# Four u tiles from TensorE to the DMA crossbar, and another order in the SyncE queue

## The chip, the cores and the metric

The kernel runs on one core of one Trainium2 chip. A core has five engines with a program each: TensorE (PE, matrix products), VectorE (DVE), ScalarE (ACT), GpSimd (POOL) and SyncE (SP). SyncE and GpSimd also issue DMAs, each from a queue of its own that works strictly in its program's order. The metric is device time in microseconds, the median over several runs. An engine waits for another through semaphores; whatever is next in its program waits behind the waiting instruction.

## The reference

A causal attention with a sliding window of 64, then a low-rank mixing along the sequence, then a two-layer MLP, both with a residual:

```python
scores = scale * np.matmul(q, k.transpose(0, 1, 3, 2))   # 8 batches, 8 heads, 576 x 64
mask = (rel >= 0) & (rel < 64)
attn = softmax(np.where(mask, scores, -1e9))
x = np.matmul(attn, v).transpose(0, 2, 1, 3).reshape(B, S, 512)
h = x.transpose(0, 2, 1) @ U @ V                          # rank 32, along the sequence
u = x + h.transpose(0, 2, 1)
out = u + np.maximum(u @ w_ch1, 0.0) @ w_ch2              # 512 -> 2048 -> 512
```

Inputs and output are float32; the kernel computes in bf16 with float32 accumulation.

## The kernel before

The 8 x 576 = 4608 tokens are seen in two ways. The attention and the mixing go by batch (576 tokens, four and a half tiles of 128). The MLP goes by chunk: nine chunks of 512 tokens, four tiles each, tile number g = 0 to 35. Batch b begins in tile g0 = floor(4.5 b), so batch 1 has its tiles t = 0 to 4 at g = 4 to 8, batch 2 has t = 0 to 3 at 9 to 12, batch 3 has t = 0 to 4 at 13 to 17. Chunk 2 is made of g = 8 to 11 (the last tile of batch 1 and three of batch 2), chunk 3 of g = 12 to 15 (the last of batch 2 and t = 0 to 2 of batch 3).

The program is one software pipeline with a schedule written out by hand. `mlp(c)` gives 32 steps for chunk c, here called groups: 16 products with W1, each 4 matmuls of 128x128 by 128x512 into a PSUM tile `psA` (line 765), whose relu goes to DVE or ACT by the lists `DVE_RELU` (775, 777); then, for each of the four output tiles, four quarters of the product with W2 into `psU` (789), a residual sum on DVE (802) and a store (815). Each group has a slot number, 0 to 31. After the group of a slot comes what the tables `PLACE...` put in that slot: the pieces of batch b = c + 1. A number above 100 means a slot of the next chunk. All engines get their instructions in that one order.

The pieces of a batch are:

- `T`: k and q with the head dimension on the partitions. Batches 0 and 1 do it on TensorE. From batch 2 on it is five `TX(t)`, each with two crossbar transposes (DMA) of SyncE, kf<-kr and qf<-qr (line 306). Their slots stand in `CROSS`: in chunk 1, for example, batch 3's at slots 10 to 14 and batch 4's at 26 to 30.
- `S`, `M`: scores (347; the short last block first, into `low` and `high`), exponential on ACT (367, 400), mask multiply on DVE (373, 380).
- `SV`: shifted copies of v, `vB`, on ACT and DVE (149, 152).
- `PV`: probabilities times v (409) and the division on DVE (490 to 512), into `xs`.
- `U`, `V`: the two low-rank products (533, 542; 660), and the sum with x on DVE (675) that gives a u tile `un`. The V product of a whole batch is made in one slot, by `mixed`: before the change in the order tile 4, tiles 0 and 1, tiles 2 and 3, and DVE sums in the same order. Tile 4 uses one bank of each of two other PSUM pools (`two_banks`).
- `UT(t)`: u with the model dimension on the partitions, `uTc`, which is what the W1 groups read. For batches below `NXT` = 3 it is four TensorE transposes into the PSUM tile `tpu` (694) and a copy on ACT (697). From batch 3 on it is one crossbar transpose on SyncE (690).

In chunks 1 and 2 the first W1 group is made in two pieces, three tiles and then the fourth, so that the last `uTc` tile may come a little later.

SyncE's queue has the transposes of k and q, those of u and the output stores, each waiting for its data in program order. GpSimd's queue has the loads of k, q and v from DRAM (128, 137), which cast float32 to bf16. `loads(b, t)` holds them back: a one-element copy `held` on GpSimd (963) reads tile t of the transposed q of batch b + 1, so that it waits for that transpose to land; behind it in the queue come the loads of v of batch b + 1 (for b = 1 and 2) and of k and q of batch b + 2. A second `held` (974), in later chunks, waits for the fourth `uTc` tile of the running chunk before the v loads of the next batch. k and q of a batch land in the buffers `kr`, `qr` that batch b - 2 had; the transposed ones in `kf`, `qf`, two of each.

Of the kernel before, what the change touches and what calls it, by code (L numbers as in the profile page):

```python
# [16 lines left out]
def kernel(  # L17
# [12 lines left out]
    B, H, S, D = q.shape  # L30
# [11 lines left out]
    NGR = 2  # L42
    NXB = 2
    NXT = 3
    FOLD = {0: 0, 1: 0, 2: 1, 3: 1}
    GP = S // GR
    NFULL = S // P
    CH = 512
    TPC = CH // P
# [32 lines left out]
    NT = 5  # L82
# [172 lines left out]
    def attention(b, spare=False):  # L255
# [11 lines left out]
        grouped = b < NGR  # L267
        folded = FOLD.get(b, 2)
        turn = [0]
# [415 lines left out]
        def UT(t):  # L685
            def f():
                g = g0 + t
                dst = uT_of(g // TPC)[:, g % TPC, :, :]
                if b >= NXT:
                    nc.sync.dma_start_transpose(out=dst, in_=u_tiles[g][:])  # L690
                    return
                tp = ps_tp.tile([P, NDC, P], BF16, name="tpu", tag="tp")
                for dc in range(NDC):
                    nc.tensor.transpose(  # L694
                        tp[:, dc, :], u_tiles[g][:, dc * P : (dc + 1) * P], ident[:]
                    )
                nc.scalar.copy(out=dst, in_=tp[:])  # L697
            return f
# [13 lines left out]
        if spare:  # L712
            pcs["L"] = [PVL(t) for t in range(2)]
            pcs["R"] = PVR
            pcs["XT"] = [XT(t, range(NDC if t < 2 else 2)) for t in range(NFULL)]
            pcs["idle"] = idle_turns
            pcs["X3"] = [XT(t, (2, 3)) for t in (2, 3)]
            pcs["HT"] = [HT((0, 1)), HT((2, 3))]
            pcs["V"] = [f for ts in ((0, 1), (2, 3), (4,)) for f in VM(ts)]
        else:  # L720
            def two_banks():
                return (
                    psum["mm"].tile([P, CH], FP32, name="psv0", tag="mm"),
                    ps_tp.tile([P, CH], FP32, name="psv1", tag="tp"),
                )

            def mixed(parts=None):
                parts = parts or [VM((NT - 1,), two_banks), VM((0, 1)), VM((2, 3))]
                for part in parts:
                    part[0]()  # L730
                for part in parts:
                    for add in part[1:]:
                        add()

            pcs["V"] = [mixed]
            if b == 1:

                def last():
                    for f in VM((NT - 1,)):
                        f()  # L740

                pcs["V"] = [lambda: mixed([VM((0, 1)), VM((2, 3))]), last]
            pcs["UT"] = [UT(t) for t in range(NT if odd else NT - 1)]
        return pcs


    DVE_RELU = {0: (7, 9, 11, 15), 1: (4, 7, 9, 10, 11, 13, 14)}
    DVE_RELU_N = (0, 1, 2, 4, 5, 6, 14)

    def mlp(c):  # L750
        uTc = uT_of(c)
        c1 = [None] * NFC

        def ch1(*ids):
            def f():
                if len(ids) == 1:
                    ps = {ids[0]: psum["mm"].tile([P, CH], FP32, name="psA", tag="mm")}
                else:
                    pair = ps_big.tile([P, 2, CH], FP32, name="psA", tag="big")
                    ps = {i: pair[:, n, :] for n, i in enumerate(ids)}  # L760
                parts = (slice(0, TPC - 1), slice(TPC - 1, TPC)) if c in (1, 2) and ids == (0,) else (slice(0, TPC),)
                for ts in parts:
                    for dc in range(NDC):
                        for i in ids:
                            nc.tensor.matmul(  # L765
                                ps[i][:, ts.start * P : ts.stop * P],
                                w1b[:, dc, i * P : (i + 1) * P],
                                uTc[:, ts, dc, :],
                                start=(dc == 0),
                                stop=(dc == NDC - 1),  # L770
                            )
                for i in ids:
                    c1[i] = c1_pool.tile([P, CH], BF16, name=f"c1_{i}")
                    if i in DVE_RELU.get(c, DVE_RELU_N):
                        nc.vector.tensor_relu(out=c1[i][:], in_=ps[i][:])  # L775
                    else:
                        nc.scalar.activation(out=c1[i][:], in_=ps[i][:], func=ACT.Relu)  # L777
            return f

        acc = {}  # L780

        def ch2(t, quarter, parts=((0, DM),)):
            def f():
                g = c * TPC + t
                for lo, hi in parts:
                    if quarter == 0 or len(parts) > 1:
                        acc[t] = psum["mm"].tile([P, DM], FP32, name="psU", tag="mm")
                    for i in range(4 * quarter, NFC if len(parts) > 1 else 4 * quarter + 4):
                        nc.tensor.matmul(  # L789
                            acc[t][:, lo:hi],  # L790
                            c1[i][:, t * P : (t + 1) * P],
                            w2b[:, i, lo:hi],
                            start=(i == 0),
                            stop=(i == NFC - 1),
                        )
                    if quarter < 3 and len(parts) == 1:
                        continue
                    if c < NLATE:
                        osb = late[c * TPC + t]
                    else:  # L800
                        osb = out_pool.tile([P, DM], FP32, name="osb")
                    nc.vector.tensor_tensor(  # L802
                        out=osb[:, lo:hi],
                        in0=acc[t][:, lo:hi],
                        in1=u_tiles[g][:, lo:hi],
                        op=ALU.add,
                    )
                    if c < NLATE:
                        stores.append(
                            lambda: nc.sync.dma_start(  # L810
                                out=outf[g * P : (g + 1) * P, :], in_=osb[:]
                            )
                        )
                        continue
                    nc.sync.dma_start(out=outf[g * P : (g + 1) * P, lo:hi], in_=osb[:, lo:hi])
            return f

        ups = [ch1(i) for i in range(NFC)]
        if c == 0:
            ups[0:2] = [ch1(0, 1), lambda: None]  # L820
            rest = [ch2(t, r) for r in range(4) for t in (0, 1)]
            return ups + rest + [ch2(t, r) for t in (2, 3) for r in range(4)]
        rest = [ch2(t, r) for t in range(TPC) for r in range(4)]
        if c == NCH - 1:
            rest[-4:] = [ch2(TPC - 1, 0, ((0, 3 * P), (3 * P, DM)))]
        return ups + rest


    PLACE = {
        "S": [0, 0, 0, 3, 3],  # L830
        "M": [0, 1, 2, 4, 5],
        "PV": [8],
        "U": [14],
        "V": [18],
        "UT": [19, 19, 20, 20, 21],
    }
    PLACE_0 = {"V": [0, 0, 1, 2, 2, 3, 4, 4, 4]}
    PLACE_1 = {
# [7 lines left out]
        "UT": [28, 29, 30, 31, 102],  # L846
    }
    PLACE_2 = {
        "S": [9, 9, 9, 12, 12],
        "M": [9, 10, 11, 13, 14],  # L850
        "SV": [15, 15, 16, 16],
        "PV": [18],
        "U": [23],
        "V": [25],
        "UT": [28, 29, 30, 31],
    }
    PLACE_3 = {**PLACE, "SV": [5, 5, 6, 6], "V": [16], "UT": [17, 17, 18, 18, 19]}
    CROSS = {
        0: {2: [16, 17, 18, 19, 20]},
        1: {3: [10, 11, 12, 13, 14], 4: [26, 27, 28, 29, 30]},  # L860
        2: {5: [24, 25, 26, 27, 28]},
    }
    CROSS_N = [22, 23, 24, 25, 26]
# [81 lines left out]
    for c in range(NCH):  # L945
        slots = all_slots[c]
# [8 lines left out]
        b = c + 1  # L955
        if b < B:
# [4 lines left out]
            def loads(b, *tiles):  # L961
                for t in tiles:
                    nc.gpsimd.tensor_copy(  # L963
                        out=held[:],
                        in_=qfs[(b + 1) % 2][0:1, t * HP * P : t * HP * P + 1],
                    )
                if b <= 2:
                    load_v(b + 1)
                for _ in load_kq(b + 2, False):
                    pass  # L970
# [5 lines left out]
            if 2 < b and b + 2 < B:  # L976
                loads(b, 2)
            where = {1: PLACE_1, 2: PLACE_2, 3: PLACE_3}.get(b, PLACE)
            if b < NXB:
# [23 lines left out]
            if b == 1:  # L1003
                slots[20].append(lambda: loads(1, 2))
            if b == 2:
                slots[15].append(lambda: loads(2, 2))
        for fill, extra in zip(mlp(c) + [lambda: None], slots):
            fill()
            if c == NCH - 2 and stores:
# [33 lines left out]
```

The softmax here doesn't subtract the row's maximum and nothing guards it: scores larger than these inputs give would overflow.

## Time and profile before

| | us |
|---|---|
| median of 13 runs | 311.18 (310.94 to 313.27) |
| the profiled execution | 310.99 |
| its span in the profile | 309.0 |
| TensorE busy | 302.3 (98%) |
| DVE / ACT / GpSimd busy | 174.4 / 108.3 / 102.0 |
| chunk 1 starts / chunk 2 / chunk 3 / chunk 4 | 59.56 / 92.64 / 124.43 / 155.99 |

The page gives the busy time of each engine, and the span in 40 slices; the chain of waits is the sequence of work that ended last, followed back from the last instruction; a timeline lists instructions of one engine with their start, their length and, in brackets, how long the engine was idle before and what ended that. A DMA's "us to landing" is counted from the start of its issue to its completion. Line numbers are those of the kernel before; in the changed kernel they are one higher from line 45 on.

### The profile page before, as it was taken

What the parts mean: (1) busy time and instruction counts of PE and PEld (TensorE: products, weight loads), DVE (VectorE), ACT (ScalarE), POOL (GpSimd) and SP (SyncE); (2) the same over time, 40 slices, a digit from 0 to 9 for tenths busy, and PEclk for the clock granted to TensorE, in tenths of its full rate; (3) what the DMA queues carried; (4) which work ended last, traced back from release to release, by engine and by line L of the source; (5) the groups of instructions that cost most, each with busy time, mean ns of one, the idle gap of its engine ahead of it and who ended that gap; (6) DMA issues with size and microseconds to landing.
All of it is one profiled execution on the core that took longest, in us unless ns stands there. A gap on an engine that the chain in (4) does not pass through costs nothing.

```text
span 309.0 us, 6974 instructions
## 1 busy us (share of the span) xinstructions
PE 302.3 (98%) x2903; PEld 147.1 (48%) x2903; DVE 174.4 (56%) x336; ACT 108.3 (35%) x173; POOL 102.0 (33%) x136
## 2 busy tenths in 40 slices
PE   7989999999999999999999999999999999999996
PEld 6643554544445544454445444544454444444443
DVE  4585467527757773677567765766566542116011
ACT  3745670458128610642054304430344004101500
POOL 8693264294399091519233705000000000000000
PEclk9999999999999999999999999999999999999999
DMA  7999999999999999999999999933300275011011
GB/s 107 165 210 208 205 171 142 158 131 156 129 150 156 135 150 148 205 152 152 155 154 116 190 129 125 179 104 85 122 2 0 68 236 192 34 68 36 0 66 69
DMA packets 156495, 39.87 MB, mean 129 GB/s; under 512 B 145040, under 2 KB 151440, under 8 KB 156464
## 3 DMA queue, kind: packets, MB, share of 16 engines
q0 software_dynamic: 104720, 18.88, 84.4%
q1 hardware_dynamic: 51744, 20.55, 36.0%
q8 instruction: 22, 0.36, 0.5%
q14 instruction: 9, 0.07, 0.1%
HBM read 37.97 MB, written 9.44 MB: 153 GB/s over the span
## 4 chain that ended last, share of the span: by engine, by line
PE 93%; DMA 3%; POOL 2%; issue 1%; DVE 0%; POOLq 0%
PE psA L765 41%; PE psU L789 41%; DMA vA<-in_v_dram 3%; PE sc L347 3%; PE xw L409 2%; PE psv L660 1%; PE pshh L533 1%; PE tpu L694 1%; PE tpg L283 0%; POOL qr L120 0%; PE low L347 0%; PE psh L533 0%; POOL vB L152 0%; PE xr L409 0%; POOL kr L120 0%
## 5 line engine op out<-in xcount | busy, mean ns | idle before, releaser
L765 PE MATMUL psA<-uTc,w1b 128*128 128x512 bf16 (+1 forms) x584 | 131.2, 377 | 0.3 <-DVE uTc L635 0.3
L789 PE MATMUL psU<-w2b,c 128*128 128x512 bf16 (+2 forms) x592 | 128.9, 373 | 0.0
L789 PEld LDWEIGHTS <-c 128*128 128x128 bf16 x592 | 56.0, 98 | 66.1 <-issue 3.1
L765 PEld LDWEIGHTS <-w1b 128*128 128x128 bf16 x584 | 54.4, 98 | 63.9 <-issue 2.6
L777 ACT ACTIVATE c<-psA 128x512 bf16<-128x512 f32 x84 | 50.0, 597 | 83.6 <-PE psA L765 83.3
L775 DVE TENSOR_SCALAR c<-psA 128x512 bf16<-128x512 f32 x60 | 41.4, 690 | 40.9 <-PE psA L765 40.9
L802 DVE TENSOR_TENSOR osb<-psU,un 128x512 f32<-128x512 f32 (+2 forms) x29 | 19.5, 671 | 51.9 <-PE psU L789 51.9
L367 ACT ACTIVATE pts<-sc 128x1024 bf16<-128x1024 f32 x32 | 31.4, 1030 | 2.4 <-PE sc L347 2.3
L138 POOL DMA_DIRECT2D vA<-in_v_dram x32 | 28.3, 912 | 7.3 <-DMA w1b<-in_moe_w_ch_dram 2.7
L675 DVE TENSOR_TENSOR un<-psv,xs 128x512 bf16<-128x512 f32 (+3 forms) x48 | 26.1, 593 | 5.5 <-PE psv L660 5.3
L129 POOL DMA_DIRECT2D qr<-in_q_dram x30 | 26.8, 895 | 3.8 <-PE sc L347 1.7
L129 POOL DMA_DIRECT2D kr<-in_k_dram x30 | 26.6, 887 | 3.5 <-PE psA L765 2.0
L400 ACT ACTIVATE ptl<-low 128x256 bf16<-128x256 f32 x6 | 2.3, 383 | 60.5 <-PE high L347 60.5
L373 DVE TENSOR_TENSOR pts<-pts,maskA 128x1024 bf16<-128x1024 bf16 x28 | 19.1, 682 | 1.7 <-ACT pts L367 1.7
L500 DVE TENSOR_TENSOR xs<-xw,rcw 128x896 bf16<-128x896 f32 x14 | 15.3, 1092 | 0.5
L963 POOL COPY held<-qf 1x1 bf16<-1x1 bf16 x5 | 0.9, 177 | 42.9 <-DMA qf<-qr 42.9
L347 PEld LDWEIGHTS <-kf 64*64 64x64 bf16 x704 | 9.9, 107 | 7.4 <-issue 6.4
L347 PE MATMUL sc<-qf,kf 64*64 64x128 bf16 (+1 forms) x608 | 11.7, 212 | 0.5 <-DVE qf L300 0.3
L409 PEld LDWEIGHTS <-pts 128*64 128x64 bf16 x512 | 9.9, 110 | 3.8 <-issue 2.9
L697 ACT COPY uTc<-tpu 128x512 bf16<-128x512 bf16 x9 | 5.3, 585 | 11.1 <-PE tpu L694 11.1
L409 PE MATMUL xw<-vA,pts 128*64 128x65 bf16 x217 | 8.4, 195 | 0.0
L138 POOL DMA_DIRECT2D vB<-in_v_dram x8 | 7.3, 907 | 2.8 <-DMA qr<-in_q_dram 2.4
(125 smaller groups left out, 180.8 us busy)
## 6 DMA issues: line engine op xcount, KB each, us to landing
out_dram<-osb SPq DMA_DIRECT2D x27, 256.0 KB, 2.4
vA<-in_v_dram POOLq DMA_DIRECT2D x32, 128.0 KB, 7.6
kr<-in_k_dram POOLq DMA_DIRECT2D x24, 128.0 KB, 5.7
qr<-in_q_dram POOLq DMA_DIRECT2D x24, 128.0 KB, 5.7
w2b<-in_moe_w_ch_dram POOLq DMA_DIRECT2D x4, 512.0 KB, 15.8
out_dram<-late SPq DMA_DIRECT2D x8, 256.0 KB, 4.1
vB<-in_v_dram POOLq DMA_DIRECT2D x8, 128.0 KB, 8.8
w1b<-in_moe_w_ch_dram POOLq DMA_DIRECT2D x2, 512.0 KB, 10.8
```

Of the source, the lines that this page charges most:

```text
L129: nc.gpsimd.dma_start(out=dst[0:rows, t, :, :], in_=src[b, :, t * P : t * P + rows, :].rearrange("h p d -> p h d"),)
L138: nc.gpsimd.dma_start(out=dst[:, :, 0:D], in_=v[b, :, lo : lo + P, :].rearrange("h p d -> p h d"))
L347: nc.tensor.matmul(sc[g][r0 : r0 + W, col * W : (col + n) * W], keys_of(j, u, rs), queries_of(j, blk, n, rs), start=not spare, stop=last o ...
L367: nc.scalar.activation(out=dst, in_=sc[:], func=ACT.Exp, scale=scale)
L373: nc.vector.tensor_tensor(out=dst, in0=dst, in1=maskA.rearrange("p g n w -> p g (n w)"), op=ALU.mult)
L409: nc.tensor.matmul(dst, pts[:, h // 2, h % 2, blk, :] if blk < NB - 1 else ptl[:, h // 2, h % 2, :], rhs, start=True, stop=True,)
L675: nc.vector.tensor_tensor(out=u_tiles[g][rs, cs], in0=ps[0][n][rs], in1=x[rs, t, :, :].rearrange("p h d -> p (h d)")[:, cs], op=ALU.add,)
L765: nc.tensor.matmul(ps[i][:, ts.start * P : ts.stop * P], w1b[:, dc, i * P : (i + 1) * P], uTc[:, ts, dc, :], start=(dc == 0), stop=(dc == ...
L775: nc.vector.tensor_relu(out=c1[i][:], in_=ps[i][:])
L777: nc.scalar.activation(out=c1[i][:], in_=ps[i][:], func=ACT.Relu)
L789: nc.tensor.matmul(acc[t][:, lo:hi], c1[i][:, t * P : (t + 1) * P], w2b[:, i, lo:hi], start=(i == 0), stop=(i == NFC - 1),)
L802: nc.vector.tensor_tensor(out=osb[:, lo:hi], in0=acc[t][:, lo:hi], in1=u_tiles[g][:, lo:hi], op=ALU.add,)
```

## The change

A table `XUT` names four u tiles below batch 3 that now take the crossbar: tile 4 of batch 1, tiles 0, 1 and 3 of batch 2. `mixed` makes tiles 0 to 3 ahead of tile 4. Batch 2's pieces move one to five slots forward in chunk 1; the `UT` of batch 3 and of later batches one slot or two. Two of batch 4's five `TX` move from slots 29 and 30 of chunk 1 to slot 17 of chunk 2, which is after the `UT` of batch 3's tiles 0 to 2 (slot 16) and before those of its tiles 3 and 4 (slot 18). `held` in chunk 1 reads tile 4 of batch 3's transposed q where it read tile 2. Chunk 2's first W1 group is made in one piece, and chunk 1's relus of DVE are others, the same in number.

```diff
+    XUT = ((1, 4), (2, 0), (2, 1), (2, 3))
...
-                if b >= NXT:
+                if b >= NXT or (b, t) in XUT:
                     nc.sync.dma_start_transpose(out=dst, in_=u_tiles[g][:])
                     return
...
-                parts = parts or [VM((NT - 1,), two_banks), VM((0, 1)), VM((2, 3))]
+                parts = parts or [VM((0, 1)), VM((2, 3)), VM((NT - 1,), two_banks)]
...
-    DVE_RELU = {0: (7, 9, 11, 15), 1: (4, 7, 9, 10, 11, 13, 14)}
+    DVE_RELU = {0: (7, 9, 11, 15), 1: (3, 6, 8, 9, 10, 12, 13)}
...
-                parts = (slice(0, TPC - 1), slice(TPC - 1, TPC)) if c in (1, 2) and ids == (0,) else (slice(0, TPC),)
+                parts = (slice(0, TPC - 1), slice(TPC - 1, TPC)) if (c, ids) == (1, (0,)) else (slice(0, TPC),)
...
     PLACE = {
...
-        "UT": [19, 19, 20, 20, 21],
+        "UT": [18, 18, 19, 19, 20],
...
     PLACE_2 = {
-        "S": [9, 9, 9, 12, 12],
-        "M": [9, 10, 11, 13, 14],
-        "SV": [15, 15, 16, 16],
-        "PV": [18],
-        "U": [23],
-        "V": [25],
-        "UT": [28, 29, 30, 31],
+        "S": [8, 8, 8, 11, 11],
+        "M": [8, 9, 10, 12, 13],
+        "SV": [13, 13, 14, 14],
+        "PV": [15],
+        "U": [20],
+        "V": [22],
+        "UT": [23, 23, 28, 25],
     }
-    PLACE_3 = {**PLACE, "SV": [5, 5, 6, 6], "V": [16], "UT": [17, 17, 18, 18, 19]}
+    PLACE_3 = {**PLACE, "SV": [5, 5, 6, 6], "V": [16], "UT": [16, 16, 16, 18, 18]}
     CROSS = {
         0: {2: [16, 17, 18, 19, 20]},
-        1: {3: [10, 11, 12, 13, 14], 4: [26, 27, 28, 29, 30]},
+        1: {3: [10, 11, 12, 13, 14], 4: [26, 27, 28, 117, 117]},
...
-                slots[15].append(lambda: loads(2, 2))
+                slots[15].append(lambda: loads(2, NT - 1))
```

## The prediction

> **What bounds the kernel now.** I read the page first, then the chain of work that ended last, then the timelines of the SyncE and GpSimd queues with the landing times of their transfers.
>
> ```profile
> span 309.0 us, 6974 instructions
> PE 302.3 (98%) x2903; PEld 147.1 (48%) x2903; DVE 174.4 (56%) x336; ACT 108.3 (35%) x173; POOL 102.0 (33%) x136
> PEclk9999999999999999999999999999999999999999
> PE 93%; DMA 3%; POOL 2%; issue 1%; DVE 0%; POOLq 0%
> ```
>
> TensorE is the bound: 98% busy, the clock full in every slice. The chain's 3% of DMA and 2% of POOL lie in the first 16 us. From 21.9 us on it is TensorE without a hole, so a matmul taken out shortens the run by its length, and a TensorE wait put in lengthens it by its length. Nothing after 22 us can absorb either.
>
> The chain, in order of time (start, us, what, instructions), has the transposes that the change removes, and the place I fear:
>
> ```profile
> 62.34 0.22 PE tpu L694 x4
> ...
> 89.16 0.22 PE tpu L694 x4
> 90.25 0.22 PE tpu L694 x4
> ...
> 92.42 0.22 PE tpu L694 x4
> ...
> 124.43 0.86 PE psA L765 x4
> 125.29 0.14 PE low L347
> ```
>
> The last two lines are the start of chunk 3: its first W1 group, then the scores of batch 4. These scores need the fourth and fifth q and k tiles of batch 4, crossbar-transposed by SyncE.
>
> The GpSimd timeline shows when transposes land, because a `held` copy waits for one and lets the next loads go:
>
> ```profile
> 82.20 0.18 POOL L963 COPY held<-qf 1x1 bf16<-1x1 bf16 x1 [9.12 <-DMA qf<-qr]
> 82.73 3.52 POOL L138 DMA_DIRECT2D vA<-in_v_dram  x4 [0.36 <-DVE rco L508]
> ...
> 107.81 0.18 POOL L963 COPY held<-qf 1x1 bf16<-1x1 bf16 x1 [7.56 <-DMA qf<-qr]
> 108.63 0.87 POOL L129 DMA_DIRECT2D kr<-in_k_dram  x1 [0.65 <-issue]
> ```
>
> And the SyncE timeline (issues; each transposed tile takes SyncE some 1.3 us):
>
> ```profile
> 83.72 1.22 SPq L306 DMA_TRANSPOSE qf<-qr  x1
> 92.04 1.19 SPq L306 DMA_TRANSPOSE kf<-kr  x1
> ...
> 99.28 1.51 SPq L306 DMA_TRANSPOSE qf<-qr  x1
> ...
> 106.39 1.78 SPq L306 DMA_TRANSPOSE qf<-qr  x1
> 112.48 6.25 SPq L690 DMA_TRANSPOSE uTc<-un  x4
> ```
>
> Now batch 4's last transpose is issued at 106.39 and lands 6.4 us later, at 112.8: 12.5 us before the scores at 125.3.
>
> How long a transpose takes depends on the loads around it. Alone it lands in 2.4 us (qf issued at 81.11). The DMA issues of a short window around 112.5 us, with the us to landing at the end:
>
> ```profile
> kr<-in_k_dram POOLq DMA_DIRECT2D x1, 128.0 KB, 6.3
> uTc<-un SPq DMA_TRANSPOSE x1, 6.3
> ```
>
> A load issued at 112.09 and a transpose issued at 112.48 took the same 6.3 us, although nothing was left before that transpose on its own queue (the last one landed at 112.8). So the transfers of both queues are served about in the order of their issue. The price of a place in that line: from the load issued at 92.27 (landed 98.9) to the transpose issued at 106.39 (landed 112.8) lie 7 full loads and 9 transposes in 13.9 us, 0.87 us each; from the load of 108.63 (landed 113.2) to the u tile of 119.42 (landed 125.4) lie 8 loads, 5 transposes and a store in 12.2 us, again 0.87.
>
> **The change, part by part.**
>
> *Four u tiles leave TensorE.* Batch 1's tile 4 and batch 2's tiles 0, 1 and 3: 4 x 0.22 us by the chain's rows = -0.88 us, all of it on the path. ScalarE loses four copies of 0.585 us that nobody waited for: nothing. Chunk 2's first W1 group is no longer split; at chunk 1 the two pieces are 4 matmuls in 0.65 us and 4 in 0.22 us, 0.87 against 0.86 for an unsplit group: nothing.
>
> *The u tiles in time?* Batch 1's tile 4 is ready at 60.4 and goes into SyncE's gap between 62.7 (last transpose of batch 2's q) and 70.5; needed at 91.8. Batch 2's attention comes three groups sooner (3 x 0.86, and 0.22 of removed transposes): its V product at 83.0 instead of 85.8, its first sums at about 83.9, before SyncE is through with batch 3's transposes at 84.9. So SyncE issues tiles 0, 1 and 3 at 85.0, 86.3 and 87.6. GpSimd's loads now start after 86.8 (below), so 2.4 to 5.0 us to landing (5.0 is the row of 83.72, which had loads beside it): tile 1 at 88.7 to 91.3, needed when chunk 2 starts, at 92.64 - 0.88 = 91.8. In time by 0.5 us at worst. Tile 2, still on TensorE, moves two groups forward. Nothing.
>
> *Batch 2's attention sooner.* Its scores start at 67.5; the last transposed q tile lands at 61.45 + 5.3 = 66.8. P times V moves 2.8 us forward, from 77.88 to 75.07, but the last mask multiply (75.41 + 0.68 = 76.1 now) moves only with its scores, one group and 0.22, to 75.0. The slack of 1.8 us is gone; between 0 and 0.3 us of wait, I take +0.1. The seven DVE relus of chunk 1 are renumbered, not added. V products in the order (0,1), (2,3), (4) leave one 128x512 bank of the "mm" pool busy some 2.5 us longer; its next user is two groups (1.7 us) and more behind DVE's 3.1 us of sums, and three banks turn: nothing.
>
> *GpSimd's gate.* `held` in chunk 1 now waits for batch 3's last q tile (issued 83.72) instead of the third (landed 82.1). With no load beside it the last one lands in 2.4 us, at 86.1; the first v load follows 0.68 us later as now, at 86.8 instead of 82.73: +4.1 us. Behind it in GpSimd's queue: five v loads of batch 3, ten q and k loads of batch 4, five v loads of batch 4, the next `held`, and q and k of batch 5. Batch 3's v then lands at 91.4 + 4.1 = 95.5; its shifts come at 98.5: covered. Batch 4's v (110.6 now) is shifted at 117: covered. But batch 4's first k load lands 4.1 us later, so SyncE's transposes of batch 4 begin at 96.1 instead of 92.04, the third q tile is issued at 103.4 and lands at 111.8 instead of 107.7, and batch 5's loads begin at 112.7 instead of 108.63.
>
> *SyncE's order in chunk 2.* Batch 4's tiles 3 and 4 (four transposes) now stand behind batch 3's u tiles 0 to 2. These wait for DVE's sums: V product at 110.72 - 0.88 = 109.8, first sum done 0.9 us later, first issue at 110.9 (before: 112.48, since the halves of tile 4 were summed first). SyncE idles from 104.9 until then. Then 1.3 us each: u tiles at 110.9, 112.2, 113.5, batch 4's k and q tiles at 114.8, 116.1, 117.4 and **118.7**. That last one went at 106.39 before.
>
> When does it land? Batch 5's loads issue from 112.7 on, 0.87 us apart, right among these. Bounds: 2.4 us (alone), at 121.1; and by the line, first load at 112.7 + 4.6 = 117.3, then 6 loads and 5 transposes of 0.87 us: 126.9. The nearest rows are the three u tiles that now go 3.9, 5.2 and 7.0 us after the first load of batch 5: they took 6.3, 7.5 and 8.1 us. The last q tile would be 6.0 us after it: 7.8 us, 126.5. I take this. The scores of batch 4 could start at 125.29 - 0.88 + 0.1 = 124.5. **TensorE waits 2.0 us** there, at the start of chunk 3, with everything of that chunk queued behind in program order. Batch 3's u tiles, which the same chunk needs at 123.7, land by 113.5 + 2.4 to 6.3, before 120: the order helps them by 4 us, which they need only by a hair (the third landed at 123.7 of 124.4).
>
> *Later chunks.* Two u tiles go before a store; they land (2.6 us) 4 us ahead of need, and the second `held` opens up to 3 us sooner, for loads needed 20 us later. Nothing.
>
> **Sum** against the profiled execution, 310.99 us (span 309.0, 2 us around it; the median of the 13 runs is 311.18): -0.88 + 0.1 + 2.0 = +1.2, **312.2 us**.
>
> [...]
>
> **Rivals.**
> 1. *No wait at batch 4's scores.* The transposes overtake the loads: the chunk's -0.88 stays, 310.2 us, faster. For it: v loads issued at 97.95 landed after 12.6 us while a transpose of the same moment (97.87) took 8.3, so in a long backlog transposes do overtake, by up to 4 us; 2 us are enough. Against it: the u tiles of 112 to 116 did not. It decides from a landing before 124.7, a latency under 6.0 us at 118.7.
> 2. *A small wait*, 0.2 to 1.4 us, landing between 124.7 and 125.9 (a latency of 6.0 to 7.2 us): within 0.2% of now, about 311.0. For it speak the u tile of 117.54, with 6.9 us, and the transposes of 92 to 95, with 5.7 to 7.3; against it, that these had fewer transposes ahead of them.
> 3. *The wait is elsewhere*: batch 2's u tile 1 late for chunk 2. If it took the 8.1 us that is the longest of any u tile, it would land at 94.4, 2.6 us late: 310.99 - 0.78 + 2.6 = 312.8. It decides from a latency of 5.4 us; the gate on the loads speaks against it.
> 4. *SyncE slower too*: the four u tiles of 112.48 took 6.25 us, 1.56 each. At that pace the last q tile goes at 120.3 and lands at 128.1: wait 3.6, 313.8 us.
>
> **How the numbers follow.** The measurement tells about 0.2% (0.6 us) from no change. Forecast, with rival 4 in it (a wait over 1.4 us at batch 4's scores): 0.55. Rival 1: 0.25. Rival 2: 0.13. Rival 3: 0.07. Slower 0.55 + 0.07 = 0.62, same 0.13, faster 0.25. The range takes in rival 1 with 0.3 us to spare below and rival 4 above, 309.9 to 313.8; the forecast alone, 311.6 to 313.8.
>
> **What would show it.** 36 - 16 = 20 TensorE transposes of u left. `held` in chunk 1 ending at 86.3, not 82.2. SyncE's last transpose of batch 4 at about 118.7. In the chain, a piece "DMA qf<-qr" or "kf<-kr" of about 2 us before the scores near 124.5. I am wrong if that piece is missing, if q's transposes under batch 5's loads land in less than 6 us, or if the gate's four microseconds are made up before batch 4's third q tile.

## The result: slower by 1.2%

The changed kernel takes **314.81 us** (median of 11 runs, 312.99 to 317.63) against 311.16 for the kernel before (48 runs in all, 310.28 to 313.27): a ratio of **1.012**, 95% interval 1.0101 to 1.0138. The prediction had the sign and the place; its 312.2 us was 2.6 us short, and the result lies above its range.

The profiled execution took 315.28 us, 4.29 more than that of before. The page after:

```profile
span 313.6 us, 6946 instructions
PE 304.0 (97%) x2883; PEld 147.0 (47%) x2883; DVE 174.7 (56%) x336; ACT 106.1 (34%) x169; POOL 101.9 (32%) x136
PEclk9999999999999999799999999999999999999999
PE 88%; DMA 7%; POOL 2%; SPq 1%; issue 1%; DVE 0%; POOLq 0%
```

TensorE has 20 instructions fewer (four transposes of four matmuls, and four matmuls of chunk 2's first group, which is no longer split), and yet is busy 1.7 us longer. The chain has 7% of DMA where it had 3%. And the clock's row, full in all 40 slices before, has a 7 in the seventeenth, which is the stretch from 125.4 to 133.3 us.

Its chain of waits (start, us, what) shows where all this lies:

```profile
61.65 6.25 DMA qf<-qr
67.94 0.19 PE low L348
...
120.86 6.91 DMA qf<-qr
127.81 0.19 PE low L348
128.13 0.46 PE sc L348 x31
128.59 4.38 PE psA L766 x12
```

Three things are new. Batch 2's scores (67.94) wait for the q tile that SyncE issued at 61.65. Batch 4's scores (127.81) wait for the q tile that SyncE issued at 120.86. And the twelve W1 matmuls behind those scores take 4.38 us. The same twelve took 2.70 in the kernel before (126.00 to 128.70 us). The waits, as a table of who waited for whom (us in total, times, longest):

```profile
PE low L348 <- DMA qf<-qr: 3.2, 2, 2.7
```

By the windows (us, busy of PE, weight load, DVE, ACT, POOL, granted clock, which is the share of full speed that TensorE was given, DMA share, GB/s) the clock was full while TensorE stood still, and low after it went on:

```profile
124.00:128.00 4.00, 1.27 (x27) 0.58 (x27) 1.38 (x2) 0.00 (x0) 2.71 (x5) 1.00 1.84 156
128.00:133.00 5.00, 5.00 (x71) 2.08 (x63) 2.97 (x5) 2.49 (x4) 1.75 (x2) 0.66 1.51 215
```

So the bill of the profiled execution is: four transposes, -0.88; wait at batch 2's scores, +0.50; wait at batch 4's scores, +2.73; twelve matmuls at the low clock, 4.38 - 2.70 = +1.68. Together +4.03 of the 4.6 by which the span is longer (the times differ by 4.29). The rest is spread: the product of the probabilities with v in chunk 1, for one, begins with a piece of 0.41 us where it has 0.34 in chunk 2. By chunks, from first W1 group to first W1 group: chunk 1 33.1 us before and 33.0 after, chunk 2 31.8 and 31.8, chunk 3 31.6 and **36.1**, and from the start of chunk 4 to the end 153.2 and 153.4.

The queues tell why the q tile was late. GpSimd's timeline:

```profile
88.37 0.18 POOL L964 COPY held<-qf 1x1 bf16<-1x1 bf16 x1 [14.28 <-DMA qf<-qr]
88.91 3.52 POOL L139 DMA_DIRECT2D vA<-in_v_dram  x4 [0.36 <-PE psU L790]
...
114.83 0.18 POOL L964 COPY held<-qf 1x1 bf16<-1x1 bf16 x1 [8.72 <-DMA qf<-qr]
115.66 0.87 POOL L130 DMA_DIRECT2D kr<-in_k_dram  x1 [0.65 <-issue]
```

and SyncE's:

```profile
114.25 1.20 SPq L691 DMA_TRANSPOSE uTc<-un  x1
115.98 2.13 SPq L307 DMA_TRANSPOSE kf<-kr  x1
118.22 1.21 SPq L307 DMA_TRANSPOSE qf<-qr  x1
...
120.86 1.46 SPq L307 DMA_TRANSPOSE qf<-qr  x1
```

Batch 5's loads start at 115.66, among the last transposes of batch 4 which now stand behind the third u tile (114.25). In the kernel before, the last q tile of batch 4 was issued at 106.39, 14.5 us sooner.

### The profile page after: what moved, and what is told of

Read it like the earlier page. It is cut to its first block, busy times and chain, and to the rows that moved or that the text cites. A ratio compares the mean times of both kernels' runs of the same rounds, so it can differ in the third digit from the quotient of the medians.

```text
span 313.6 us, 6946 instructions
## 1 busy us (share of the span) xinstructions
PE 304.0 (97%) x2883; PEld 147.0 (47%) x2883; DVE 174.7 (56%) x336; ACT 106.1 (34%) x169; POOL 101.9 (32%) x136
## 4 chain that ended last, share of the span: by engine, by line
PE 88%; DMA 7%; POOL 2%; SPq 1%; issue 1%; DVE 0%; POOLq 0%
PE psA L766 39%; PE psU L790 38%; DMA qf<-qr 4%; DMA vA<-in_v_dram 3%; PE sc L348 2%; PE xw L410 2%; PE psv L661 1%; SPq L307 1%; PE pshh L534 1%; PE tpg L284 0%; POOL qr L121 0%; PE low L348 0%; PE psh L534 0%; POOL vB L153 0%; PE tpu L695 0%
## 5 line engine op out<-in xcount | busy, mean ns | idle before, releaser
L766 PE MATMUL psA<-uTc,w1b 128*128 128x512 bf16 (+1 forms) x580 | 132.7, 382 | 0.3 <-DVE uTc L636 0.3
L778 ACT ACTIVATE c<-psA 128x512 bf16<-128x512 f32 x84 | 50.0, 597 | 84.4 <-PE psA L766 84.1
L803 DVE TENSOR_TENSOR late<-psU,un 128x512 f32<-128x512 f32 x8 | 5.4, 687 | 6.1 <-PE psU L790 6.1
```

The costliest lines, as they stand in the source:

```text
L766: nc.tensor.matmul(ps[i][:, ts.start * P : ts.stop * P], w1b[:, dc, i * P : (i + 1) * P], uTc[:, ts, dc, :], start=(dc == 0), stop=(dc == ...
L803: nc.vector.tensor_tensor(out=osb[:, lo:hi], in0=acc[t][:, lo:hi], in1=u_tiles[g][:, lo:hi], op=ALU.add,)
```

## Experiments

All are edits of the changed kernel unless the text says otherwise; each was timed against the kernel before on the same chip.

### Is the order in SyncE's queue the cause, and was it needed?

The order of before for batch 4's transposes, everything else as changed:

```diff
-        1: {3: [10, 11, 12, 13, 14], 4: [26, 27, 28, 117, 117]},
+        1: {3: [10, 11, 12, 13, 14], 4: [26, 27, 28, 29, 30]},
```

> The changed kernel, but batch 4's last two transposed tiles stand in SyncE's queue where they stood before (slots 29 and 30 of chunk 1), ahead of batch 3's u tiles. Theory: the 2.73 us wait for batch 4's last q tile at the start of chunk 3, and with it the slow TensorE clock of the 5 us after it (12 matmuls in 4.38 us instead of 2.70), are gone, because that tile is issued by about 112 and has 12 us to land; what remains is -0.88 for four transposes and +0.5 for the wait at batch 2's scores: 310.5 to 311.0 us. Rival, that the order was needed: with the gate late, batch 3's third u tile then lands after 124 and chunk 3 waits for it instead: 312 us or more.

Measured: 312.2 us (310.6 to 315.07), ratio 1.0031 (0.9994 to 1.0069). Batch 4's scores wait for nothing; chunk 3's first W1 group does, which is what the rival said. Chain of this kernel:

```profile
116.51 7.79 DMA uTc<-un
124.31 1.34 issue
125.64 1.02 PE psA L766 x4
```

The view stops here at the second u tile of batch 3. SyncE's issues of batch 3's u tiles are at 115.10, 116.51 and 118.88; the third landed 6.7 us after its issue, at 125.6, which is the moment at which TensorE goes on after 2.1 us of standing still. In the changed kernel the third was issued at 114.25. So the order does what it says: in the changed kernel the u tiles come sooner. And the time goes to whichever transfers are put behind: 2.1 us here, 2.73 there. What makes them late together must lie ahead of both. By the medians this version is 2.6 us faster than the changed kernel although its wait is only 0.6 us shorter: in this execution the clock stayed full after it (1.00 from 124 to 133 us), and batch 2's scores did not wait either. Its other executions show the clock as a cost of its own: the three of ten with a mean clock of 0.993 to 0.995 took 314.23 to 315.07 us, the seven with 0.998 to 1.000 took 310.6 to 312.36.

### Is the later gate needed?

`held` in chunk 1 waits for tile 2 again, as before the change:

```diff
-                slots[15].append(lambda: loads(2, NT - 1))
+                slots[15].append(lambda: loads(2, 2))
```

> The changed kernel, but the held copy of chunk 1 waits for the third q tile of batch 3 again, so that the loads behind it start about 4 us sooner. Theory: SyncE still issues batch 4's last q tile at about 119 to 121, for it stands behind batch 3's u tiles, but batch 5's loads are by then mostly done; it lands in 5 to 6 us, at 125, and the wait at chunk 3 falls from 2.73 to between 0 and 1 us, with no slow clock: 311 to 312 us, with a wait of up to 1 us for batch 2's second u tile at chunk 2's start because loads run beside it. Rival, that the order alone makes the wait: it stays over 2 us and the time over 314.

A miss: measured 319.5 us (317.87 to 320.58), ratio 1.0234 (1.0177 to 1.0292), the slowest version of the change. With the gate open at 84.4 us, batch 3's v loads meet batch 2's u tiles:

```profile
88.08 7.38 DMA uTc<-un
...
95.70 1.87 PE psA L766 x4
...
97.92 0.85 PE sc L348 x24
98.77 4.00 PE psA L766 x12
```

Tile 1 of batch 2 took 7.4 us beside the loads (in the changed kernel, issued at 88.40, it took 3.6), chunk 2 waits 3.17 us for it, and then the group, the scores and the twelve matmuls run at a granted clock of 0.61 (95.5 to 103 us): 1.87 for 0.86, 0.85 for 0.46, 4.00 for 2.70, together +2.7. With 1.0 us at batch 2's scores and the -0.88 that is +6.0 of the 7.2 us by which the span is longer than before. This is the prediction's third rival, brought about by taking away the gate that spoke against it. At batch 4's scores the theory was right: they wait for nothing here (the last q tile lands at 130.67, the scores start at 131.5). It also shows that the change's gate is what brings the new crossbar tiles in on time, and the gate in turn is what pushes batch 4's transposes and batch 5's loads back.

### The gate alone

The kernel before with that one line of the change (`loads(2, NT - 1)`):

> The kernel before with the one line of the gate changed (held in chunk 1 waits for batch 3's fifth q tile). Theory: batch 4's transposes and batch 5's loads come 4 us later, but all of batch 4's transposes still stand ahead of batch 3's u tiles and land by about 117, 8 us before their scores; the u tiles are issued about 1 us later and land no later than now: within 0.3 us of the kernel before, 311.2. Rival, that the gate by itself costs: batch 3's third u tile, which now lands 0.7 us before chunk 3 needs it, lands after 124.4 and the time rises by 1 to 3 us.

Measured: 311.82 us (310.82 to 313.66), ratio 1.0011 (0.9985 to 1.0037), no difference that can be told. The last q tile of batch 4 is issued at 111.34 there, 5 us later than before, and is still in time. No wait for a transfer shows in its profiled execution, and by the interval the delay by itself costs 1.2 us at most. That the slack which it uses up is what the reordering then needs is argued from these runs, not tested alone.

### The order alone

The kernel before with the change's order in SyncE's queue and of the sums, without the crossbar tiles, the gate and batch 2's move:

```diff
-                parts = parts or [VM((NT - 1,), two_banks), VM((0, 1)), VM((2, 3))]
+                parts = parts or [VM((0, 1)), VM((2, 3)), VM((NT - 1,), two_banks)]
...
-    PLACE_3 = {**PLACE, "SV": [5, 5, 6, 6], "V": [16], "UT": [17, 17, 18, 18, 19]}
+    PLACE_3 = {**PLACE, "SV": [5, 5, 6, 6], "V": [16], "UT": [16, 16, 16, 18, 18]}
...
-        1: {3: [10, 11, 12, 13, 14], 4: [26, 27, 28, 29, 30]},
+        1: {3: [10, 11, 12, 13, 14], 4: [26, 27, 28, 117, 117]},
```

> The kernel before with SyncE's new order alone: batch 4's last two transposed tiles behind batch 3's first three u tiles, and the V products with tile 4 last so that these u tiles are ready sooner; the gate on the loads and all u tiles of batches 1 and 2 are left as they were. Theory (the wait comes from the order and the late loads together): batch 5's loads begin near 108.6 as before, batch 4's last q tile is issued at 119 to 121, when few of these loads are left, and lands in 4 to 6 us; the scores at 125.3 wait 0 to 1.2 us, TensorE's clock stays full: 311.2 to 312.4. Rival, that the order alone makes the whole wait: 2.7 us and the slow clock, 315.

Measured: 313.59 us (311.04 to 316.11), ratio 1.0055 (1.0024 to 1.0086), above what was expected. Its profiled execution (312.02) has the wait at batch 4's scores, but a short one; chain and waits:

```profile
121.36 4.54 DMA qf<-qr
...
126.72 2.70 PE psA L765 x12
```

```profile
PE low L347 <- DMA qf<-qr: 0.4, 1, 0.4
```

So the reordering alone can make these scores wait, even with the early gate. The median is 1.6 us above the profiled execution; what the longer executions waited for was not seen, but it was not the clock alone: two of 313.65 and 314.04 us have a mean clock of 1.000.

### Was it batch 5's loads?

The order of the change is kept; only batch 5's loads are moved, behind batch 4's last q tile:

```diff
             if 2 < b and b + 2 < B:
-                loads(b, 2)
+                if b == 3:
+                    slots[18].append(lambda: loads(3, NT - 1))
+                else:
+                    loads(b, 2)
```

> The changed kernel with the same order in SyncE's queue, but batch 5's loads of q and k held until batch 4's last q tile has landed, so that they cannot stand before it. Theory: that tile is still issued at 118 to 120, but lands in 2.4 to 3.5 us, by 123; chunk 3 starts without a wait and with a full clock, batch 5's data come some 8 us later and are still 20 us early: the changed kernel's gain less the 0 to 0.5 us at batch 2's scores, 310.3 to 310.9. Rival, that SyncE's issue and the transposes themselves are too slow: the wait stays over 2 us, 314 or more.

Measured: 311.97 us (310.45 to 312.51), ratio 1.0007 (0.9991 to 1.0023; by the medians, with 311.07 for the kernel before in this comparison, 0.9 us slower): of the 3.6 us that the change lost, most are back. The transfer in question, in a DMA view of the moment of its issue (119.50), with the us to landing at the end; and below it the same in the changed kernel (issue 120.86):

```profile
qf<-qr SPq DMA_TRANSPOSE x1, 2.4
```

```profile
qf<-qr SPq DMA_TRANSPOSE x1, 6.9
```

The same transpose, with the same ones ahead of it on its queue, takes 2.4 us without the loads and 6.9 with them: the loads make it late. The prediction read out of two rows of 6.3 us that both queues are served about in the order of issue. In the changed kernel the landings agree with it, which is as far as the runs show: the six loads issued from 115.66 to 120.02 and the four transposes issued from 115.98 to 120.86 land, from 121.27 to 127.87, in the order of their issue, but for the last two, which are 0.1 us apart. From the first landing to the q tile's that is 0.72 us a place, where the prediction took 0.87. Chunk 3 now has no wait at all. But batch 5's loads begin at 122.89, and the delay comes up one chunk on:

```profile
149.11 7.64 DMA uTc<-un
...
156.89 1.02 PE psA L766 x4
```

A u tile of batch 4 lands 1.64 us late for chunk 4. The gain of 0.88 us is paid back there.

### The clock after the wait

A cover of twelve matmuls on idle data stands in TensorE's queue before batch 4's scores, so that TensorE works while it waits:

```diff
+        if c == 3:
+
+            def cover():
+                spin = psum["mm"].tile([P, CH], FP32, name="spin", tag="mm")
+                for _ in range(12):
+                    nc.tensor.matmul(spin[:], idle[:, 0:P], idle[:], start=True, stop=True)
+
+            slots[0].append(cover)
```

> The changed kernel with 12 idle matmuls of 512 columns (about 2.6 us) put into TensorE's queue between chunk 3's first group and batch 4's scores, where it waits anyway. Theory: the wait for the transposed tile stays as long (the scores still start when it lands, near 127.8 in the profile) but TensorE is not idle, its clock stays full, and the 12 matmuls after the scores take 2.70 us and not 4.38: 1.3 to 1.7 us faster than the changed kernel, 313.1 to 313.5. Rival, that the slow matmuls come from DMA traffic or anything but the idle time: no change, 314.8.

Measured: 313.7 us (313.03 to 314.68), ratio 1.0062 (1.0035 to 1.0089), 1.1 us below the changed kernel by the medians, with more work on TensorE. Chain, and the window that answers to the one with 0.66:

```profile
121.23 7.61 DMA qf<-qr
128.88 0.19 PE low L348
...
129.66 2.70 PE psA L766 x12
```

```profile
128.00:133.00 5.00, 4.12 (x101) 2.37 (x101) 2.76 (x5) 3.04 (x6) 0.87 (x1) 1.00 1.58 214
```

The scores start 1.1 us later than in the changed kernel and the twelve matmuls are nevertheless done sooner. The slow clock is a cost of its own, and here, where the cover left 1.24 us of idle time, it did not come. Nine of the ten executions have a mean clock of 0.998 or more, one (314.56 us) has 0.993. The wait at batch 2's scores is not there in this execution (nor in those of most other versions), so its 0.50 us is not part of every run.

### How long a wait brings the slow clock?

In the kernel before, a matmul after the first group of chunks 5, 6, 7 and 8 needs the last of 2, 3, 4 and 5 copies on ScalarE, which makes four waits of growing length:

```diff
+    spin = const.tile([P, CH], BF16, name="spin")
+    WAITS = {5: 2, 6: 3, 7: 4, 8: 5}
...
+                if c in WAITS and ids == (0,):
+                    for _ in range(WAITS[c]):
+                        nc.scalar.copy(out=spin[:], in_=c1[0][:])
+                    sink = psum["mm"].tile([P, CH], FP32, name="sink", tag="mm")
+                    nc.tensor.matmul(sink[:], spin[:, 0:P], idle[:], start=True, stop=True)
```

> What a wait of TensorE costs, by itself: the kernel before with an idle matmul after the first group of chunks 5, 6, 7 and 8, which needs the last of 2, 3, 4 and 5 ScalarE copies in a row, the first of which needs that group's relu. Nothing else is changed; by the chain (relu 0.69, copies of some 0.4 to 0.6 us) TensorE waits about 1.7, 2.2, 2.7 and 3.3 us. Theory: the slow matmuls after the changed kernel's wait of 2.73 us come from the wait, so chunks with waits over about 2.5 us have 12 or so matmuls after it at 0.6 to 0.7 of the clock, some 1.7 us more, and those under 2.1 us none. Rival, that they came from the transfers of that stage: chunks 7 and 8 have no loads or transposes, and show waits without slow matmuls; the time is then 311.2 plus the four waits.

Measured: 328.87 us (327.81 to 330.0), ratio 1.0568. TensorE's timeline gives the waits in the brackets:

```profile
190.83 0.39 PE L784 MATMUL sink<-idle,spin 128*128 128x512 bf16 x1 [2.08 <-ACT spin L782]
227.20 0.39 PE L784 MATMUL sink<-idle,spin 128*128 128x512 bf16 x1 [2.79 <-ACT spin L782]
262.58 0.39 PE L784 MATMUL sink<-idle,spin 128*128 128x512 bf16 x1 [3.44 <-ACT spin L782]
296.38 0.39 PE L784 MATMUL sink<-idle,spin 128*128 128x512 bf16 x1 [4.09 <-ACT spin L782]
```

A wait of 2.08 us brought the slow clock (twelve matmuls in 4.14 us) and one of 2.79 did not (2.70). So neither theory stands as written: there is no length from 2.08 to 4.09 us above which it came in this run, and chunk 8, where hardly a transfer runs (DMA share 0.03 around the wait), had it too.

In these traces the slow clock goes by where the wait falls. The record of the granted clock in the traces has two values, 1.00 and 0.50, and from one change to the next lie whole multiples of 3.413 us: 54, 1, 20, 1, 9, 1 and 8 of them here, 36, 1 and 53 in the changed kernel. Cut at these points, the windows (columns as above) around the first, the second and the fourth wait of this run read:

```profile
188.18:191.59 3.41, 1.32 (x46) 0.61 (x48) 1.12 (x2) 1.31 (x3) 2.38 (x3) 1.00 1.66 131
191.59:195.00 3.41, 3.41 (x35) 1.38 (x24) 1.45 (x3) 2.42 (x4) 0.00 (x0) 0.50 1.93 127
...
222.31:225.72 3.41, 2.10 (x10) 0.77 (x8) 1.38 (x2) 0.50 (x1) 0.00 (x0) 1.00 0.57 219
225.72:229.13 3.41, 1.93 (x58) 1.18 (x59) 0.43 (x1) 2.60 (x6) 0.00 (x0) 1.00 0.06 19
...
293.99:297.40 3.41, 1.02 (x5) 0.51 (x6) 0.00 (x0) 2.24 (x4) 0.00 (x0) 1.00 0.03 5
297.40:300.82 3.42, 3.42 (x10) 1.22 (x8) 1.38 (x2) 0.00 (x0) 0.00 (x0) 0.50 0.00 0
```

And around the wait at batch 4's scores in the changed kernel:

```profile
125.57:128.98 3.41, 1.17 (x55) 0.86 (x55) 0.36 (x2) 0.81 (x3) 1.72 (x3) 1.00 1.83 156
128.98:132.39 3.41, 3.41 (x10) 1.21 (x9) 2.24 (x5) 1.69 (x2) 1.17 (x2) 0.50 1.45 242
132.39:135.80 3.41, 3.41 (x50) 1.70 (x49) 1.88 (x5) 2.43 (x3) 0.00 (x0) 1.00 1.61 147
```

Ahead of each slow window stands one in which TensorE was busy for only 1.32, 1.02 and 1.17 us. The wait of 2.79 us fell across a border and left 2.10 in one window and 1.93 in the next, and the clock stayed full. It is so in all twelve traces, up to the last matmul. Six windows at full clock had TensorE idle for 2.03 us or more (1.38 us busy at most, in the run with the gate taken back), and each was followed by a window at half the clock. In no other was it idle for more than 1.86 us (1.56 busy, in the run with the order of before), and none of them was. One slow window was followed by another: in the run with the gate taken back, where TensorE was idle for 1.1 us of the first. Worked out from 3.413 us at 0.50, a slow window costs 1.7 us at most: that is the 1.68 of the changed kernel, and the 1.7 by which the sixty matmuls after the third and the fourth wait exceed 60 x 0.216 us (14.64 against 13.0). It came almost without transfers too: the DMA share is 0.03 in the window from 293.99 and 0.00 in the one from 297.40.

The first border lies at 4.71 us of the span in the kernel before, at 6.10 in the changed kernel and at 7.3 here, so it has no fixed place in the span. That the executions of one program differ because a wait falls otherwise in the windows is the author's reading: one execution of each was traced. As an estimate, one slow window takes 3.413 / 2 us off some 313, which is 0.0055 of the mean clock, so that the mean tells how many there were (0.994 in the profiled execution of the changed kernel, whose trace has one before the last matmul). In the run with the four waits two executions show 0.984, the traced one with its three slow windows among them, and the other two 0.988 and 0.989, which is two windows by this estimate. Of the changed kernel's eleven timed executions three show 1.000 (312.99, 313.51 and 314.34 us), seven 0.993 to 0.995, which is one slow window, and one 0.988, which is two (317.63). As an estimate from the windows above, a wait of 2.73 us that falls anywhere has 2 us or more in one window in (3.41 + 2.73 - 2 x 2.0) / 3.41, some six of ten executions.

### A version without the waits?

The last three versions keep the order of before, and hold batch 5's loads until batch 4's last q tile is there:

```diff
-        1: {3: [10, 11, 12, 13, 14], 4: [26, 27, 28, 117, 117]},
+        1: {3: [10, 11, 12, 13, 14], 4: [26, 27, 28, 29, 30]},
...
-                loads(b, 2)
+                loads(b, NT - 1 if b == 3 else 2)
```

> The changed kernel with batch 4's last two transposed tiles back in front of batch 3's u tiles (as in the run that did only this, whose third u tile landed at 124.3 and kept chunk 3 waiting 2.1 us), and batch 5's loads held until batch 4's last q tile has landed instead of its third. Theory: these loads begin at 117 to 121 instead of 115; the u tiles, issued from 112 to 117, meet fewer of them and the third lands by 121; no wait at chunk 3: 310.3 to 311. Rival, that the u tiles are late because of their place alone: 312 as in that run.

Measured: 311.57 us (310.5 to 314.3), ratio 1.001 (0.9988 to 1.0033). No wait in chunk 3 (the tile that landed at 124.3 in the earlier run was its second; the one waited for, the third, landed at 125.6). Instead, as with the loads moved above, the u tile for chunk 4 is late:

```profile
149.67 7.85 DMA uTc<-un
157.66 1.02 PE psA L766 x4
```

TensorE waited 2.56 us there, and the clock stayed full (1.00 from 155 to 165 us): 1.0 us of the wait lay in one window of 3.41 us and 1.5 in the next.

Next, the same with all of batch 2's pieces one slot later, so that its scores have more slack:

```diff
-        "S": [8, 8, 8, 11, 11],
-        "M": [8, 9, 10, 12, 13],
-        "SV": [13, 13, 14, 14],
-        "PV": [15],
-        "U": [20],
-        "V": [22],
-        "UT": [23, 23, 28, 25],
+        "S": [9, 9, 9, 12, 12],
+        "M": [9, 10, 11, 13, 14],
+        "SV": [14, 14, 15, 15],
+        "PV": [16],
+        "U": [21],
+        "V": [23],
+        "UT": [24, 24, 29, 26],
```

> The kernel of the run with batch 4's tiles in front and batch 5's loads held longer, and all pieces of batch 2 one slot later in chunk 1. Theory: batch 2's scores, which in the changed kernel waited 0.5 us for the last q tile (landed at 67.9), then start 0.86 us later than that tile needs and wait no more, and u tiles 0, 1 and 3 lose nothing, for SyncE reaches them only when it is through with batch 3: 0.2 to 0.5 us faster than without the shift, 310.2 to 310.5. Rival, that the second u tile is then late for chunk 2: no faster, or slower.

Measured: 311.19 us (310.67 to 314.81), ratio 1.0005 (0.998 to 1.003). Its profiled execution waits for no transfer in chunks 1 to 4, but for ScalarE: the probabilities' product with v stands behind the third shifted copy of v, which ScalarE makes after a relu. Chain:

```profile
76.30 0.60 ACT c L778
76.93 0.63 ACT vB L150
77.60 0.42 PE xw L410 x14
```

0.6 us of the 0.88 go there. So that copy was put one slot sooner:

```diff
-        "SV": [14, 14, 15, 15],
+        "SV": [14, 14, 14, 15],
```

> The kernel of the run with batch 4's tiles in front, batch 5's loads held longer and batch 2 one slot later, with one more edit: ScalarE's third shifted copy of batch 2's v goes ahead of chunk 1's last relu. In that run's profile no transfer kept TensorE waiting, but the product with v of batch 2 waited for this copy until 77.6 and chunk 1 took 32.94 us, 0.14 less than before, where four removed transposes alone are worth 0.88. Theory: ScalarE's copy (0.6 us behind the relu) is where the rest went; chunk 1 then takes 32.3 to 32.5 us, 310.4 to 310.8 in all, faster than both kernels. Rival, that VectorE or the next step of batch 2 is as late: no change, 311.1.

Measured: **310.48 us** (310.06 to 314.25), ratio **0.9976** (0.9967 to 0.9985): faster than both kernels, by 0.7 us of the 0.88 that the transposes are worth. Chain:

```profile
75.62 0.35 PE xw L410 x14
...
149.84 7.80 DMA uTc<-un
157.77 1.87 PE psA L766 x4
```

The product with v follows without a gap. The profiled execution is the longest of its runs (314.25): it has the wait at chunk 4 still, 2.76 us for a u tile, and the group behind it takes 1.87 us instead of 0.86. It is 3.8 us longer than the median; the wait and half of the 2.78 us for which TensorE was busy in the slow window behind it make 4.2. The other eleven executions have a mean clock of 0.998 and more, so no slow window; whether the wait is shorter in them was not seen. No run has these edits without the crossbar tiles, so that the 0.7 us are the transposes' is argued from TensorE's 98%, not shown.

## Why the prediction was right and wrong

- **The gain**, four transposes at 0.22 us: right. 20 of 36 TensorE instructions of u's transposes are left.
- **The u tiles in time**: right, by less than said. Tile 1 of batch 2 was issued at 88.40 (86.3 predicted) and landed at 92.04, in 3.6 us (2.4 to 5.0). Chunk 2 started at 92.3 and not at 91.8, so part of the margin is luck: the wait at batch 2's scores gave it. The third rival's mechanism is real: with the gate taken back it was worth 3.2 us of wait and 2.7 of slow clock.
- **Batch 2's scores**, no wait: wrong by 0.50 us in this execution. The last q tile was issued at 61.65 and took 6.25 us (61.45 and 5.3 predicted); the margin was 0.7 us, and the 6.3 us that the prediction quotes for two other transfers would have used it up. For the product of the probabilities with v 0.1 was taken and 0.07 measured.
- **The gate**: +4.1 us predicted, +6.2 measured (88.37 instead of 82.20). The last q tile took 2.4 us, as taken; SyncE issued it at 85.78 instead of 83.72. Its five pairs began at 71.82 instead of 70.53 and lost 0.8 more on the way, which the prediction had left as it was. Part of this differs from run to run: in the seven other versions with this gate `held` began at 86.65 to 87.32, some 4.5 to 5.1 us later than before.
- **SyncE's order**: mechanism right, and the latency nearly (6.9 us for 7.8 predicted). The issue was at 120.86, not 118.7: 0.7 us because the first u tile went at 111.63 and not at 110.9, 0.4 because batch 4's first k tile behind them went late (115.98), and 0.9 because its issue took 2.13 us where 1.3 was taken. So the landing was at 127.77 instead of 126.5, and **the wait 2.73 us instead of 2.0**. The first rival (transposes overtake the loads) is refuted by its own sign, a latency under 6.0 us. The second rival, a small wait, is what the order alone gave (0.4 us in its profiled execution).
- **The sum** is where it failed, first by its price of a wait. It took a TensorE wait at its length: "a TensorE wait put in lengthens it by its length". The slow clock after the wait was in no term and in no rival, and cost 1.68 us in the profiled execution. It is shown by the window at 0.50, and by the cover, with which the clock stayed at 1.00. With the other terms as predicted and 1.7 us added, the forecast would have been 313.9 us. Then come two sizes: the wait was 0.73 longer than its term, and the 0.50 at batch 2's scores had none. With them it is 315.1, and 315.28 was measured. The three executions without a slow window, 312.99 to 314.34 us, are what such sizes cost at a full clock.
- **The fourth rival** (SyncE slower, 313.8 us) was the nearest, but by luck: it took 1.56 us for each issue, and the u tiles went 1.3 us apart. The last q tile did go at 120.86 where it said 120.3, for the reasons above, and landed at 127.77 where it said 128.1. The slow clock was not in it.

## What to carry to other kernels

Here a queue that was fed late carried the delay on: a lateness of the same kind stood at batch 4's scores (2.73 us), at chunk 3's u tile (2.1) or at chunk 4's u tile (1.64 to 2.76), depending on which transfer was put last, and only moving loads out of the way and giving back slack in the pieces ahead of them turned the change into a gain. When a saving makes several engines' queues start later, write down for every transfer behind it when it is issued, what lies beside it and when it is needed, one chunk further than the edit. And a wait of a saturated TensorE is not priced by its length alone: the changed kernel paid 2.73 us for the wait and 1.68 for the slow window behind it, in which the clock was at 0.50 for 3.413 us (the gate taken back had two such windows, 2.7 us). The cost came in some executions and not in others: by their mean clock in eight of the changed kernel's eleven. Where a wait can't be avoided, independent matmuls in front of it may keep the clock: with twelve of them here nine of ten executions kept it, at a mean clock of 0.998 or more.

## What the runs showed that was not expected

- The clock after a wait was not a matter of its length alone. After 2.08 us twelve matmuls took 4.14 us instead of 2.70, after 2.79 they took 2.70. In the twelve traces here, idle time of 2.03 us or more within one window of 3.413 us was followed by a window at half the clock, and up to 1.86 us was not.
- The same 512-column crossbar transpose lands in 2.4 us alone, and in the changed kernel in 5.9 to 9.1 us between 98.9 and 124 us, where GpSimd's loads are under way. A reordering of SyncE's queue alone moved which of them is late; in the pair compared with and without the loads, 6.9 and 2.4 us, these decided whether it was.
- Executions of one program fall apart by the clock: with the order of before put back, 310.6 to 312.36 us at a mean clock of 0.998 and more, 314.23 to 315.07 at 0.993 to 0.995. The changed kernel had a slow window in eight of its eleven.
